# Moving batch 2's u transposes from TensorE to the DMA crossbar in a fused attention and mixer kernel

## The chip, the cores and the metric

The kernel runs on one core of one Trainium2 chip. The metric is the device time of one execution in microseconds (us), measured several times. A profiled execution gives a trace as well. A run counts as "slow" when it is over 1.5% above the fastest of the same kernel, else as "fast"; nearly all runs here are fast, and single runs are of unknown state. The granted clock of the core is recorded with each run; the text names it where a run of a changed kernel had 0.995 or less. The rounds ran on several chips, and the kernel before was timed anew in each.

Engines in the profile: PE is TensorE (matmuls), PEld its weight loads, DVE is VectorE, ACT is ScalarE, POOL is GpSimd, SP is SyncE. Here SP only issues DMAs; "SPq" and "POOLq" are the queues from which SP and GpSimd issue them. L748 is line 748 of the kernel.

## The reference, cut to what matters

The eight batches have 576 tokens of 512 features (8 heads of 64). First comes causal attention with a window of 64, then a low-rank mixer over the sequence, then a two-layer perceptron over the features:

```python
# attention of each batch and head, window 64, then x = heads side by side
xt = x.transpose(0, 2, 1)
h  = xt @ U @ V                       # rank 32, along the sequence
u  = x + h.transpose(0, 2, 1)         # (8, 576, 512)
ch = np.maximum(u @ w_ch1, 0.0) @ w_ch2   # 512 -> 2048 -> 512
return (u + ch).astype(np.float32)
```

In the kernels here the first product of the perceptron reads u with features on the partitions, that is, each 128x512 tile of u transposed.

## The kernel before: the parts that matter

The 8 x 576 tokens are cut into nine chunks of 512 tokens (four tiles of 128). A chunk is a list of 32 slots of perceptron work on PE: slots 0 to 15 each make one 128-row piece of the first product (`ch1`), slots 16 to 31 a quarter of one tile of the second (`ch2`). A slot is about 0.87 us of PE. Between slots, PE does the attention of a later batch; tables say after which slot each part goes. In chunk 1 this is batch 2, and its u (tiles 9 to 12) is read by chunk 2 (tiles 8 to 11) and chunk 3 (tile 12 onwards).

```python
    NXT = 3            # from this batch on, u is transposed by the crossbar
    ...
        def UT(t):
            def f():
                g = g0 + t
                dst = uT_of(g // TPC)[:, g % TPC, :, :]
                if b >= NXT:
                    nc.sync.dma_start_transpose(out=dst, in_=u_tiles[g][:])
                    return
                tp = ps_tp.tile([P, NDC, P], BF16, name="tpu", tag="tp")
                for dc in range(NDC):
                    nc.tensor.transpose(
                        tp[:, dc, :], u_tiles[g][:, dc * P : (dc + 1) * P], ident[:]
                    )
                nc.scalar.copy(out=dst, in_=tp[:])
            return f

```

`UT` either issues a crossbar transpose from SP or makes four PE transposes into the one-buffer PSUM pool `ps_tp`, with a copy on ACT. Batches 0 to 2 use PE in this kernel.

```python
        def ch1(*ids):
            def f():
                if len(ids) == 1:
                    ps = {ids[0]: psum["mm"].tile([P, CH], FP32, name="psA", tag="mm")}
                else:
                    pair = ps_big.tile([P, 2, CH], FP32, name="psA", tag="big")
                    ps = {i: pair[:, n, :] for n, i in enumerate(ids)}
                parts = (slice(0, TPC - 1), slice(TPC - 1, TPC)) if (c, ids) == (1, (0,)) else (slice(0, TPC),)
                for ts in parts:
                    for dc in range(NDC):
                        for i in ids:
                            nc.tensor.matmul(
                                ps[i][:, ts.start * P : ts.stop * P],
                                w1b[:, dc, i * P : (i + 1) * P],
                                uTc[:, ts, dc, :],
                                start=(dc == 0),
                                stop=(dc == NDC - 1),
                            )
                for i in ids:
                    c1[i] = c1_pool.tile([P, CH], BF16, name=f"c1_{i}")
                    if i in DVE_RELU.get(c, DVE_RELU_N):
                        nc.vector.tensor_relu(out=c1[i][:], in_=ps[i][:])
                    else:
                        nc.scalar.activation(out=c1[i][:], in_=ps[i][:], func=ACT.Relu)
            return f

        acc = {}
```

```python
    PLACE_2 = {                     # batch 2, in the slots of chunk 1
        "S": [9, 9, 9, 12, 12],     # scores, exp on ACT
        "M": [9, 10, 11, 13, 14],   # masks on DVE
        "SV": [15, 15, 16, 16],     # shifted copies of v on ACT and DVE
        "PV": [18],                 # values
        "U": [23],                  # x @ U
        "V": [24],                  # ... @ V, and u = x + h on DVE
        "UT": [27, 28, 29, 30],     # u transposed, tiles 9, 10, 11, 12
    }
    CROSS = {                       # q and k of a batch, transposed by the crossbar (SP)
        0: {2: [16, 17, 18, 19, 20]},
        1: {3: [10, 11, 12, 13, 14], 4: [26, 27, 28, 29, 30]},
        ...
```

In the traces here SP issues its DMAs in the order of the program (in u2, below, a u tile from a V product at 85.02 us went out at 98.64, behind four transposes that stand before it). The loads of q, k and v are issued by GpSimd and cast to bf16. In chunk 1 they are held until a crossbar transpose of batch 3 has landed (in the profile of the kernel before, GpSimd stands 8.91 us for it, until 81.92 us):

```python
            def loads(b, *tiles):
                for t in tiles:          # GpSimd copies one element, so it waits
                    nc.gpsimd.tensor_copy(out=held[:], in_=qfs[(b + 1) % 2][0:1, ...])
                if b <= 2:
                    load_v(b + 1)        # batch 3's v ...
                for _ in load_kq(b + 2, False):
                    pass                 # ... then batch 4's k and q
            ...
            if b == 2:
                slots[15].append(lambda: loads(2, 2))
```

The softmax here doesn't subtract the row's maximum and nothing guards it: scores larger than these inputs give would overflow.

Of the kernel before, what the change touches and what calls it, by code (L numbers as in the profile page):

```python
# [16 lines left out]
def kernel(  # L17
# [12 lines left out]
    B, H, S, D = q.shape  # L30
# [10 lines left out]
    GR = 6  # L41
    NGR = 2
    NXB = 2
    NXT = 3
    GP = S // GR
    NFULL = S // P
    CH = 512
    TPC = CH // P
# [199 lines left out]
    def uT_of(c):  # L248
        if c not in uT_tiles:
            uT_tiles[c] = uT_pool.tile([P, TPC, NDC, P], BF16, name="uTc")  # L250
        return uT_tiles[c]


    def attention(b, spare=False):
# [389 lines left out]
# [6 lines that stand above are left out]
# [53 lines left out]
        return pcs  # L703


    DVE_RELU = {0: (7, 9, 11, 15), 1: (4, 7, 9, 10, 11, 13, 14)}
    DVE_RELU_N = (0, 1, 2, 4, 5, 6, 8)

    def mlp(c):
        uTc = uT_of(c)  # L710
        c1 = [None] * NFC
# [5 lines that stand above are left out]
                else:  # L717
                    pair = ps_big.tile([P, 2, CH], FP32, name="psA", tag="big")
                    ps = {i: pair[:, n, :] for n, i in enumerate(ids)}
                parts = (slice(0, TPC - 1), slice(TPC - 1, TPC)) if (c, ids) == (1, (0,)) else (slice(0, TPC),)  # L720
                for ts in parts:
                    for dc in range(NDC):
                        for i in ids:
# [17 lines that stand above are left out]
        def ch2(t, quarter, parts=((0, DM),)):  # L741
            def f():
                g = c * TPC + t
                for lo, hi in parts:
                    if quarter == 0 or len(parts) > 1:
                        acc[t] = psum["mm"].tile([P, DM], FP32, name="psU", tag="mm")
                    for i in range(4 * quarter, NFC if len(parts) > 1 else 4 * quarter + 4):
                        nc.tensor.matmul(  # L748
                            acc[t][:, lo:hi],
                            c1[i][:, t * P : (t + 1) * P],  # L750
                            w2b[:, i, lo:hi],
                            start=(i == 0),
                            stop=(i == NFC - 1),
                        )
                    if quarter < 3 and len(parts) == 1:
                        continue
                    if c < NLATE:
                        osb = late[c * TPC + t]
                    else:
                        osb = out_pool.tile([P, DM], FP32, name="osb")  # L760
                    nc.vector.tensor_tensor(  # L761
                        out=osb[:, lo:hi],
                        in0=acc[t][:, lo:hi],
                        in1=u_tiles[g][:, lo:hi],
                        op=ALU.add,
                    )
                    if c < NLATE:
                        stores.append(
                            lambda: nc.sync.dma_start(
                                out=outf[g * P : (g + 1) * P, :], in_=osb[:]  # L770
                            )
                        )
                        continue
                    nc.sync.dma_start(out=outf[g * P : (g + 1) * P, lo:hi], in_=osb[:, lo:hi])
            return f

        ups = [ch1(i) for i in range(NFC)]
        if c == 0:
            ups[0:2] = [ch1(0, 1), lambda: None]
            rest = [ch2(t, r) for r in range(4) for t in (0, 1)]  # L780
            return ups + rest + [ch2(t, r) for t in (2, 3) for r in range(4)]
        rest = [ch2(t, r) for t in range(TPC) for r in range(4)]
        if c == NCH - 1:
            rest[-4:] = [ch2(TPC - 1, 0, ((0, 3 * P), (3 * P, DM)))]
        return ups + rest
# [19 lines left out]
        "UT": [28, 29, 30, 31, 102],  # L805
    }
    PLACE_2 = {
        "S": [9, 9, 9, 12, 12],
        "M": [9, 10, 11, 13, 14],
        "SV": [15, 15, 16, 16],  # L810
        "PV": [18],
        "U": [23],
        "V": [24],
        "UT": [27, 28, 29, 30],
    }
    PLACE_3 = {**PLACE, "SV": [5, 5, 6, 6]}
    CROSS = {
# [182 lines left out]
```

## Time and profile before

| | before |
|---|---|
| time, median of 3 (lowest to highest) | 312.85 us (312.75 to 312.92) |
| span in the profile | 311.4 us |
| PE busy | 303.9 us, 98% |
| chain of waits | 93% PE |
| chunk 2's first matmul | 92.67 us |

The page's first part gives the span, then busy time, share of the span and number of instructions for each engine:

```profile
span 311.4 us, 6970 instructions
...
PE 303.9 (98%) x2897; PEld 148.4 (48%) x2919; DVE 161.8 (52%) x308; ACT 108.8 (35%) x173; POOL 101.7 (33%) x133
```

The second view is the list of PE's waits between 59 and 125 us, where chunks 1 and 2 lie. Its columns are engine and line, what was waited for, total us, times, longest:

```profile
PE psU L748 <- issue: 0.2, 1, 0.2
```

PE waits for nothing there but 0.2 us of its own issue. So the kernel gets faster only by taking work from PE, and any new wait of PE counts in full.

The timeline (start, duration, engine, line, operation, how many) shows what one group of PE transposes costs. Groups of four second-layer matmuls with transposes between them start 1.085 us apart (1.09 us from 88.54 to 89.63, and the same twice more until 91.80); four such matmuls alone take 0.865 us:

```profile
88.32 0.39 PE L653 MATMUL tpu<-ident,un 128*128 128x128 bf16 x4
88.54 1.03 PE L748 MATMUL psU<-w2b,c 128*128 128x512 bf16 x4
89.41 0.39 PE L653 MATMUL tpu<-ident,un 128*128 128x128 bf16 x4
89.63 1.03 PE L748 MATMUL psU<-w2b,c 128*128 128x512 bf16 x4
...
91.80 1.03 PE L748 MATMUL psU<-w2b,c 128*128 128x512 bf16 x4
92.67 0.59 PE L724 MATMUL psA<-uTc,w1b 128*128 128x512 bf16 x2
```

SP's timeline shows when its queue is taken. The last q/k transpose of batch 3 goes out at 83.16. Batch 3's u, which already uses the crossbar here, goes out from 112.93:

```profile
83.16 1.22 SPq L304 DMA_TRANSPOSE qf<-qr  x1
...
112.93 5.89 SPq L649 DMA_TRANSPOSE uTc<-un  x4
```

Landing times (issue to the DMA's completion) are given by the view of one tile in a window. First the k transpose issued at 81.86, just before GpSimd's first load of the next group (82.46); then batch 3's u, issued from 112.93 to 119.5 beside GpSimd's loads:

```profile
L304 SPq DMA_TRANSPOSE kf<-kr x1: 1207/1207/1207, 81.9 to 81.9; - x1
...
DMA to landing us min/median/max: 2.5/2.5/2.5
```

```profile
DMA to landing us min/median/max: 6.4/7.4/8.0
```

GpSimd's timeline tells when those loads begin in chunk 1. Batch 3's v starts at 82.46 (four loads) and 85.93, and batch 4's k and q follow at once:

```profile
82.46 3.52 POOL L137 DMA_DIRECT2D vA<-in_v_dram  x4 [0.36 <-DVE rco L506]
85.93 0.92 POOL L137 DMA_DIRECT2D vB<-in_v_dram  x1
86.79 0.93 POOL L128 DMA_DIRECT2D kr<-in_k_dram  x1
```

### The profile page before, as it was taken

How to read it: one execution, taken by the hardware profiler on the slowest of the kernel's cores; microseconds unless marked ns; L12 is line 12 of the kernel's file. 1: busy time of each engine (PE TensorE's matmuls, PEld its weight loads, DVE VectorE, ACT ScalarE, POOL GpSimd, SP SyncE). 2: the span in 40 equal slices, each digit the busy share in tenths (PEclk: the TensorE clock that was granted, in tenths of full speed). 3: DMA queues.
4: the chain of work that ended last, by engine and by line, in shares of the span. 5: the costliest groups of instructions: out<-in, count | busy, mean ns of one | idle time of the engine just before them, and what ended most of it. 6: DMA issues, size and time to landing. Idle time of an engine off the chain costs nothing.

```text
span 311.4 us, 6970 instructions
## 1 busy us (share of the span) xinstructions
PE 303.9 (98%) x2897; PEld 148.4 (48%) x2919; DVE 161.8 (52%) x308; ACT 108.8 (35%) x173; POOL 101.7 (33%) x133
## 2 busy tenths in 40 slices
PE   8989999999999999999999999999999999999996
PEld 7643554544455544453445344544454444444443
DVE  4665467437758753774368435844574343016011
ACT  3745670467038510642063304340345003201500
POOL 8693263293497097029308710000000000000000
PEclk9999999999999999999999999999999999999999
DMA  7999999999999999999999999515100545010012
GB/s 108 167 210 208 205 168 147 145 148 154 129 150 140 126 152 156 182 161 159 163 155 207 150 106 181 128 48 133 69 2 0 120 180 193 27 76 34 0 64 73
DMA packets 156496, 39.88 MB, mean 128 GB/s; under 512 B 145040, under 2 KB 151440, under 8 KB 156464
## 3 DMA queue, kind: packets, MB, share of 16 engines
q0 software_dynamic: 104720, 18.88, 87.3%
q1 hardware_dynamic: 51744, 20.55, 35.0%
q8 instruction: 23, 0.38, 0.5%
q14 instruction: 9, 0.07, 0.1%
HBM read 37.97 MB, written 9.44 MB: 152 GB/s over the span
## 4 chain that ended last, share of the span: by engine, by line
PE 93%; DMA 3%; POOL 2%; issue 1%; ACT 0%; DVE 0%; POOLq 0%
PE psA L724 41%; PE psU L748 40%; DMA vA<-in_v_dram 3%; PE sc L345 3%; PE xw L407 2%; PE psv L619 2%; PE pshh L531 1%; PE tpu L653 1%; PE tpg L281 0%; POOL qr L119 0%; PE low L345 0%; PE psh L531 0%; POOL vB L151 0%; PE xr L407 0%; POOL kr L119 0%
## 5 line engine op out<-in xcount | busy, mean ns | idle before, releaser
L724 PE MATMUL psA<-uTc,w1b 128*128 128x512 bf16 (+1 forms) x580 | 131.2, 378 | 0.4 <-ACT uTc L599 0.4
L748 PE MATMUL psU<-w2b,c 128*128 128x512 bf16 (+2 forms) x572 | 127.5, 373 | 1.3 <-issue 0.3
L748 PEld LDWEIGHTS <-c 128*128 128x128 bf16 x592 | 56.0, 98 | 66.4 <-issue 3.6
L724 PEld LDWEIGHTS <-w1b 128*128 128x128 bf16 x580 | 54.1, 98 | 64.4 <-issue 2.9
L736 ACT ACTIVATE c<-psA 128x512 bf16<-128x512 f32 x84 | 50.0, 597 | 88.3 <-PE psA L724 88.0
L761 DVE TENSOR_TENSOR osb<-psU,un 128x512 f32<-128x512 f32 (+2 forms) x29 | 19.5, 672 | 69.3 <-PE psU L748 69.3
L734 DVE TENSOR_SCALAR c<-psA 128x512 bf16<-128x512 f32 x60 | 41.3, 688 | 25.6 <-PE psA L724 25.6
L634 DVE TENSOR_TENSOR un<-psv,xs 128x512 bf16<-128x512 f32 (+3 forms) x48 | 26.1, 592 | 23.5 <-PE psv L619 23.3
L365 ACT ACTIVATE pts<-sc 128x1024 bf16<-128x1024 f32 x32 | 31.4, 1028 | 2.3 <-PE sc L345 2.3
L137 POOL DMA_DIRECT2D vA<-in_v_dram x32 | 28.5, 915 | 8.1 <-DMA w1b<-in_moe_w_ch_dram 2.8
L128 POOL DMA_DIRECT2D qr<-in_q_dram x30 | 26.7, 890 | 4.5 <-DMA w2b<-in_moe_w_ch_dram 3.1
L128 POOL DMA_DIRECT2D kr<-in_k_dram x30 | 26.7, 890 | 4.1 <-PE psA L724 2.0
L398 ACT ACTIVATE ptl<-low 128x256 bf16<-128x256 f32 x6 | 2.3, 384 | 62.0 <-PE high L345 62.0
L371 DVE TENSOR_TENSOR pts<-pts,maskA 128x1024 bf16<-128x1024 bf16 x28 | 19.1, 682 | 1.7 <-ACT pts L365 1.7
L922 POOL COPY held<-qf 1x1 bf16<-1x1 bf16 x5 | 1.1, 228 | 54.0 <-DMA qf<-qr 54.0
L498 DVE TENSOR_TENSOR xs<-xw,rcw 128x896 bf16<-128x896 f32 x14 | 15.3, 1091 | 0.5
L345 PEld LDWEIGHTS <-kf 64*64 64x64 bf16 x704 | 9.9, 107 | 7.7 <-issue 7.0
L345 PE MATMUL sc<-qf,kf 64*64 64x128 bf16 (+1 forms) x608 | 11.7, 212 | 0.5 <-DVE qf L298 0.3
L407 PEld LDWEIGHTS <-pts 128*64 128x64 bf16 x512 | 9.9, 110 | 3.7 <-issue 3.2
L546 ACT CAST hh<-pshh 128x512 bf16<-128x512 f32 x7 | 4.1, 586 | 13.7 <-PE pshh L539 13.5
L656 ACT COPY uTc<-tpu 128x512 bf16<-128x512 bf16 x9 | 5.3, 585 | 10.2 <-PE tpu L653 10.2
L407 PE MATMUL xw<-vA,pts 128*64 128x65 bf16 x217 | 8.4, 195 | 0.0
(115 smaller groups left out, 175.3 us busy)
## 6 DMA issues: line engine op xcount, KB each, us to landing
out_dram<-osb SPq DMA_DIRECT2D x27, 256.0 KB, 2.3
vA<-in_v_dram POOLq DMA_DIRECT2D x32, 128.0 KB, 8.1
kr<-in_k_dram POOLq DMA_DIRECT2D x24, 128.0 KB, 5.8
qr<-in_q_dram POOLq DMA_DIRECT2D x24, 128.0 KB, 6.4
w2b<-in_moe_w_ch_dram POOLq DMA_DIRECT2D x4, 512.0 KB, 15.0
out_dram<-late SPq DMA_DIRECT2D x8, 256.0 KB, 3.0
vB<-in_v_dram POOLq DMA_DIRECT2D x8, 128.0 KB, 12.3
w1b<-in_moe_w_ch_dram POOLq DMA_DIRECT2D x2, 512.0 KB, 11.5
```

The costliest lines, as they stand in the source:

```text
L128: nc.gpsimd.dma_start(out=dst[0:rows, t, :, :], in_=src[b, :, t * P : t * P + rows, :].rearrange("h p d -> p h d"),)
L137: nc.gpsimd.dma_start(out=dst[:, :, 0:D], in_=v[b, :, lo : lo + P, :].rearrange("h p d -> p h d"))
L345: nc.tensor.matmul(sc[g][r0 : r0 + W, col * W : (col + n) * W], keys_of(j, u, rs), queries_of(j, blk, n, rs), start=not spare, stop=last o ...
L365: nc.scalar.activation(out=dst, in_=sc[:], func=ACT.Exp, scale=scale)
L371: nc.vector.tensor_tensor(out=dst, in0=dst, in1=maskA.rearrange("p g n w -> p g (n w)"), op=ALU.mult)
L407: nc.tensor.matmul(dst, pts[:, h // 2, h % 2, blk, :] if blk < NB - 1 else ptl[:, h // 2, h % 2, :], rhs, start=True, stop=True,)
L634: nc.vector.tensor_tensor(out=u_tiles[g][rs, cs], in0=ps[0][n][rs], in1=x[rs, t, :, :].rearrange("p h d -> p (h d)")[:, cs], op=ALU.add,)
L724: nc.tensor.matmul(ps[i][:, ts.start * P : ts.stop * P], w1b[:, dc, i * P : (i + 1) * P], uTc[:, ts, dc, :], start=(dc == 0), stop=(dc == ...
L734: nc.vector.tensor_relu(out=c1[i][:], in_=ps[i][:])
L736: nc.scalar.activation(out=c1[i][:], in_=ps[i][:], func=ACT.Relu)
L748: nc.tensor.matmul(acc[t][:, lo:hi], c1[i][:, t * P : (t + 1) * P], w2b[:, i, lo:hi], start=(i == 0), stop=(i == NFC - 1),)
L761: nc.vector.tensor_tensor(out=osb[:, lo:hi], in0=acc[t][:, lo:hi], in1=u_tiles[g][:, lo:hi], op=ALU.add,)
```

## The change

The intent is to take batch 2's sixteen transposes off PE. The transposes then go through SP and need some microseconds to land (batch 3's u tiles took 6.4 to 8.0 us in the profile before), so batch 2's attention is moved forward in chunk 1: scores by one slot, values and both low-rank products by three, and the u transposes to slots 22 and 23, ahead of batch 4's q/k transposes (slot 26 on) in SP's order. Chunk 2's first product is split so that the first three tiles need not wait for the fourth. The fourth tile of chunk 2 is batch 2's third u tile, tile 11.

```diff
--- before.py
+++ after.py
@@ -41,7 +41,7 @@
     GR = 6
     NGR = 2
     NXB = 2
-    NXT = 3
+    NXT = 2
     GP = S // GR
     NFULL = S // P
     CH = 512
@@ -703,7 +703,7 @@
         return pcs
 
 
-    DVE_RELU = {0: (7, 9, 11, 15), 1: (4, 7, 9, 10, 11, 13, 14)}
+    DVE_RELU = {0: (7, 9, 11, 15), 1: (3, 6, 8, 9, 10, 12, 13)}
     DVE_RELU_N = (0, 1, 2, 4, 5, 6, 8)
 
     def mlp(c):
@@ -717,7 +717,7 @@
                 else:
                     pair = ps_big.tile([P, 2, CH], FP32, name="psA", tag="big")
                     ps = {i: pair[:, n, :] for n, i in enumerate(ids)}
-                parts = (slice(0, TPC - 1), slice(TPC - 1, TPC)) if (c, ids) == (1, (0,)) else (slice(0, TPC),)
+                parts = (slice(0, TPC - 1), slice(TPC - 1, TPC)) if c in (1, 2) and ids == (0,) else (slice(0, TPC),)
                 for ts in parts:
                     for dc in range(NDC):
                         for i in ids:
@@ -805,13 +805,13 @@
         "UT": [28, 29, 30, 31, 102],
     }
     PLACE_2 = {
-        "S": [9, 9, 9, 12, 12],
-        "M": [9, 10, 11, 13, 14],
-        "SV": [15, 15, 16, 16],
-        "PV": [18],
-        "U": [23],
-        "V": [24],
-        "UT": [27, 28, 29, 30],
+        "S": [8, 8, 8, 11, 11],
+        "M": [8, 9, 10, 12, 13],
+        "SV": [13, 13, 14, 14],
+        "PV": [15],
+        "U": [20],
+        "V": [21],
+        "UT": [22, 22, 23, 23],
     }
     PLACE_3 = {**PLACE, "SV": [5, 5, 6, 6]}
     CROSS = {
```

## The prediction

> **What bounds the kernel now.** TensorE. The page gives PE 303.9 us busy of a 311.4 us span (98%), at full granted clock in all 40 slices; the chain of waits is 93% PE. From chunk 0 on nothing makes PE wait: in the waits of 56 to 135 us the largest wait of a PE matmul is 0.2 us. So the time changes only by PE work removed or by a new hole in PE.
>
> **Removed.** For batch 2, sixteen 128x128 PE transposes and four ACT copies (585 ns each). In the timeline, groups of four second-layer matmuls with a transpose group between them start 1.085 us apart (88.54, 89.63, 90.72, 91.80) against 0.865 us for four such matmuls alone. So a group costs PE 0.22 us, four of them **0.88 us**, all on the critical path. The ACT copies are off it.
>
> **Added.** Four crossbar transposes on the SP queue, about 1.47 us of queue each (four of batch 3's took 5.89 us). Splitting chunk 2's first product (384 + 128 columns) costs almost nothing: the split one in chunk 1 runs as fast; I allow 0.05 us.
>
> **Moved.** Scores and masks one slot sooner, values, first low-rank product and V product three, relus one. The shift copies of v then end close to where the values start on PE (about 75 us); I allow 0.1 us.
>
> **The new critical question: do the transposes land before chunk 2 starts?** V's product moves from 85.07 to about 82.5 us, so the first u tile of batch 2 is added at about 84.1. But SP issues batch 3's ten q/k transposes back to back until 84.4, so batch 2's u goes out at about 84.5, 85.9, 87.4 and 88.9. Chunk 2 needs the first two for its first part, the third for its second; without PE's transposes it would start at 92.67 - 0.88 = 91.8. Landing takes 2.5 us [...] (the k transpose at 81.86), but GpSimd's loads of batch 4 begin at 82.46 and fill the engines from about 85: the q transpose of 83.16 took 5.4, and batch 3's u at 112.9 to 117.3, in the like situation, took 6.4, 7.0, 8.0, 7.4. [...] My estimate is 6, 6.5, 7: landings at 90.5, 92.4, 94.4. PE then stalls about 0.6 us for the second tile, runs the 0.65 us first part, and stalls another 1.0 us or so for the third. About 1.5 us (0 to 3) lost against 0.88 saved.
>
> Later: batch 4's loads and transposes are pushed by 1 to 2 us of DMA work; they have about 8 us before chunk 3 reads them. Batch 3's u transposes have 1.6 us of slack; they should just hold.
>
> **Time.** 312.85 - 0.88 + 0.05 + 0.1 + 1.3 (stall, weighed slightly low) = **313.4 us**, 8 in 10 within **312.0 to 314.7**. Faster by over 2%: 0.01; within 2%: 0.98; slower by over 2%: 0.01.
>
> **What would show it.** Right: the transpose group falls from 36 matmuls to 20; the u transposes on SP rise from 23 to 27, the new ones issued from about 84.5 us, just behind batch 3's, landing in 5.5 to 8 us; new PE waits for a DMA at chunk 2's first product, 1 to 2 us together. Wrong: landings near 4 us and no PE wait there (then 312.0).
>
> **What would make it wrong.** Landings faster or slower by 1 us move the result by up to 2 us; a later u add on DVE; batch 3's u transposes delayed enough to stall chunk 3.

312.85 - 0.88 + 0.05 + 0.1 + 1.3 = 313.42, stated as 313.4 us. The landings of 6, 6.5 and 7 us stay the estimate from the measured 6.4 to 8.0 us. In the trace of the kernel before, the transpose that took 2.5 us went out at 81.86 us and GpSimd's next load at 82.46; the time of all packets over that of 16 engines was 0.48 from 81.0 to 82.5 us, 0.44 to 84.0, 0.87 to 85.0 and 1.84 to 86.0.

## The result, and the profile after

| | before | after |
|---|---|---|
| time, median of 6 (lowest to highest) | 312.88 us (312.75 to 313.72) | 314.87 us (314.58 to 315.13) |
| ratio of the fast runs | | 1.0059, 95% interval 1.0046 to 1.0072 |
| span of the profiled execution | 311.4 us | 312.9 us |
| chunk 1, first matmul to chunk 2's first | 33.36 us | 33.32 us |
| chunk 2, the same | 32.04 us | 33.49 us |
| each of chunks 3 to 6 | 32.04 to 32.05 us | 32.04 to 32.05 us |

A ratio is the mean time of one kernel's fast runs over that of the other's of the same rounds, so it is not quite the ratio of the medians quoted. A chunk's time is the distance between the first matmuls of two chunks in the trace. The sum of chunks 1 and 2 is 65.40 us before and 66.81 after: +1.41 us. Nothing after chunk 2 differs. Another 0.24 us lies after the last DVE addition (2.72 us to the span's end before, 2.96 after), which no view explains. It belongs to the program and not to one run: in all twelve traces of kernels with NXT = 2 this end takes 2.95 to 2.97 us, in those of u1 and u8 (NXT = 3) 2.71 and 2.72, in u12 and u13 2.60 and 2.59. Chunk 1 began 0.16 us earlier in this trace, so the spans differ by 1.5 us.

The page:

```profile
span 312.9 us, 6954 instructions
...
PE 303.2 (97%) x2886; PEld 147.4 (47%) x2907; DVE 161.6 (52%) x308; ACT 106.5 (34%) x169; POOL 101.4 (32%) x133
```

PE's u transposes fell from 36 matmuls to 20 and the u transposes on SP rose from 23 to 27, as forecast. PE's waits between 59 and 125 us now have a new first line. PE waited twice for a transposed u tile:

```profile
PE psA L724 <- DMA uTc<-un: 1.9, 2, 1.3
```

PE's timeline shows both waits in brackets. V's product is at 82.42. The second layer of chunk 1 ends, then PE stands until tiles 9 and 10 have landed, runs the first part (384 columns), and stands again for tile 11:

```profile
82.42 0.71 PE L619 MATMUL psv<-hh,vrep 64*128 64x256 bf16 x6
83.06 8.81 PE L748 MATMUL psU<-w2b,c 128*128 128x512 bf16 x39
92.47 0.81 PE L724 MATMUL psA<-uTc,w1b 128*128 128x384 bf16 x4 [0.59 <-DMA uTc<-un]
94.56 0.38 PE L724 MATMUL psA<-uTc,w1b 128*128 128x128 bf16 x4 [1.28 <-DMA uTc<-un]
```

The bracketed waits understate the loss, because ends of matmuls are modelled and weight loads wait too (those of L724 stood 2.6 us between 90 and 96 us). The chunk times give it better. Without waits, chunk 1 would take 33.36 - 0.88 (transposes gone) + 0.11 (the earlier placement, measured below) = 32.59 us; it took 33.32, so the first wait cost 0.73. Chunk 2 took 33.49 against 32.04, so the second cost 1.45. The sum is 2.18 us, and -0.88 + 0.11 + 2.18 = 1.41, by construction. The starts of the matmuls check it: the holes are 0.97 and 1.61 us from one start to the next, where 0.22 and 0.16 us are usual, so 0.75 and 1.45 us too long.

SP's timeline: batch 2's u goes out immediately behind batch 3's last q transpose:

```profile
82.88 1.22 SPq L304 DMA_TRANSPOSE qf<-qr  x1
84.19 5.54 SPq L649 DMA_TRANSPOSE uTc<-un  x4
94.24 1.19 SPq L304 DMA_TRANSPOSE kf<-kr  x1
```

The landing of the u tiles (three of the four are recorded):

```profile
DMA to landing us min/median/max: 6.7/7.5/8.1
```

The chain of waits between 80 and 96 us (start, us, what) runs from the additions on DVE over SP's queue to the DMA that ends the second wait:

```profile
83.08 2.80 DVE un L634 x5
...
86.48 0.40 SPq L649
...
86.98 7.54 DMA uTc<-un
...
94.56 0.38 PE psA L724 x4
```

And GpSimd's loads, in the same place as before (those of k and q follow from 86.13):

```profile
81.80 3.52 POOL L137 DMA_DIRECT2D vA<-in_v_dram  x4 [0.36 <-PE pshh L539]
```

### The profile page after: what moved, and what is told of

It reads as the page before. It is cut to its first block, busy times and chain, and to the rows that moved or that the text cites. A ratio compares the mean times of both kernels' runs of the same rounds, so it can differ in the third digit from the quotient of the medians.

```text
span 312.9 us, 6954 instructions
## 1 busy us (share of the span) xinstructions
PE 303.2 (97%) x2886; PEld 147.4 (47%) x2907; DVE 161.6 (52%) x308; ACT 106.5 (34%) x169; POOL 101.4 (32%) x133
## 4 chain that ended last, share of the span: by engine, by line
PE 89%; DMA 5%; POOL 2%; DVE 1%; issue 1%; ACT 0%; SPq 0%; POOLq 0%
PE psA L724 41%; PE psU L748 37%; DMA vA<-in_v_dram 3%; PE sc L345 2%; DMA uTc<-un 2%; PE xw L407 2%; PE psv L619 2%; PE pshh L531 1%; DVE un L634 1%; PE tpg L281 0%; POOL qr L119 0%; PE low L345 0%; PE psh L531 0%; POOL vB L151 0%; PE tpu L653 0%
## 5 line engine op out<-in xcount | busy, mean ns | idle before, releaser
L724 PE MATMUL psA<-uTc,w1b 128*128 128x512 bf16 (+1 forms) x584 | 131.3, 377 | 2.3 <-DMA uTc<-un 1.9
L724 PEld LDWEIGHTS <-w1b 128*128 128x128 bf16 x584 | 54.3, 98 | 66.7 <-issue 5.5
L137 POOL DMA_DIRECT2D vB<-in_v_dram x8 | 7.2, 896 | 6.4 <-DMA kr<-in_k_dram 3.6
L761 DVE TENSOR_TENSOR late<-psU,un 128x512 f32<-128x512 f32 x8 | 5.4, 686 | 6.9 <-PE psU L748 6.8
```

Of the source, the lines that this page charges most:

```text
L137: nc.gpsimd.dma_start(out=dst[:, :, 0:D], in_=v[b, :, lo : lo + P, :].rearrange("h p d -> p h d"))
L724: nc.tensor.matmul(ps[i][:, ts.start * P : ts.stop * P], w1b[:, dc, i * P : (i + 1) * P], uTc[:, ts, dc, :], start=(dc == 0), stop=(dc == ...
L761: nc.vector.tensor_tensor(out=osb[:, lo:hi], in0=acc[t][:, lo:hi], in1=u_tiles[g][:, lo:hi], op=ALU.add,)
```

## The experiments

The theory ("landing"): PE waits for the landing of tiles 10 and 11, and the landing takes 7 us because GpSimd's loads are under way beside it. Rival 1 ("placement"): the earlier attention and the split cost PE time through DVE and ACT. Rival 2 ("queue"): a u transpose takes 7 us anyway, so only the late issue matters. All kernels gave correct results. Each was timed in 5 rounds against the kernel before, except where said; with the profiled run that makes six times (five for u10). "Chunks 1+2" is from the trace, to be compared with 65.40 us before and 66.81 after.

### u1: PE transposes again, everything else of the change kept

```diff
-    NXT = 2
+    NXT = 3
```

> The change with batch 2's u transposed by PE again (placement and split kept). Landing theory (PE waits for the crossbar at chunk 2's start): no wait for a DMA there, 312.9 us, ratio 1.000 within 0.001. Rival (earlier placement and split cost PE time through DVE, ACT or shorter matmuls): stays well slower than before, near 314.9 plus 0.9 of transposes, about 315.7.

Measured: 315.29 us (315.04 to 315.61), before 313.16, ratio 1.0058 (1.0029 to 1.0086). Chunks 1+2: 67.39 us. This missed the expectation, and taken alone it would have favoured rival 1. PE's timeline shows why it is no clean undo:

```profile
84.44 0.40 PE L653 MATMUL tpu<-ident,un 128*128 128x128 bf16 x4
85.51 0.38 PE L653 MATMUL tpu<-ident,un 128*128 128x128 bf16 x4 [0.67 <-ACT uTc L656]
```

The same comes again at 86.60 and 87.66.

Two groups of transposes stand in one slot. The second needs the only buffer of `ps_tp`, which ACT has to empty first, so PE waits 0.67 us twice in the brackets; from group start to group start it is 1.07 us, against 0.22 us for a group. Undoing one part left the others arranged for something else. So the run does not decide between the theories; u8 is the mended version.

### u8: PE transposes in their old slots, attention early, product split

```diff
-    NXT = 2
+    NXT = 3
-        "UT": [22, 22, 23, 23],
+        "UT": [27, 28, 29, 30],
```

> The earlier placement of batch 2's attention and the split alone: the u transposes back on PE and in their old slots (27 to 30), where the first such run had put them right behind V's product and PE waited for the additions and for the single PSUM buffer. Landing theory: nothing of the loss is left, 312.9 to 313.1 us (0.1 us for the placement). Rival (the placement costs): still 314 or more.

Measured: 313.17 us (312.94 to 315.83; the slowest at a granted clock of 0.995), before 313.26, ratio 1.0012 (0.9986 to 1.0037). Chunks 1+2: 65.51 us, 0.11 more than before, and no wait of PE for a DMA. So the placement and the split together cost 0.11 us. Rival 1 falls.

### u2: the crossbar alone, old placement, no split

```diff
-    NXT = 3          # in the kernel before
+    NXT = 2
```

> The kernel before with the crossbar for batch 2's u only: old placement, no split. Landing theory: V's product stays at about 85 us, so the u transposes are issued from about 86.7 and the third, that the unsplit first product needs, lands at about 89.7 + 7 = 96.7, against 91.6 for PE: stall 5 us, less 0.9 saved, so about 317 us. Rival (placement and split are what costs): 312.0 to 312.5.

Measured: 334.49 us (333.91 to 335.51, granted clock 0.967 to 0.969), before 313.16, ratio 1.0673. The direction was the landing theory's, the size four times its 5 us. PE waited 19.7 us in one piece:

```profile
PE psA L724 <- DMA uTc<-un: 19.7, 1, 19.7
```

SP's timeline shows what the expectation had overlooked. In the old slots 27 to 30 the u transposes (L649) stand in SP's program in turn with batch 4's q/k transposes (L304), behind the first two pairs of them, and those wait for batch 4's loads:

```profile
95.46 1.41 SPq L304 DMA_TRANSPOSE kf<-kr  x1
96.96 1.59 SPq L304 DMA_TRANSPOSE qf<-qr  x1
98.64 1.31 SPq L649 DMA_TRANSPOSE uTc<-un  x1
100.05 1.32 SPq L304 DMA_TRANSPOSE kf<-kr  x1
```

V's product was at 85.02 us, but the first u tile went out at 98.64 and the third at 107.71. In this trace SP stood 7.6 us at the first of batch 4's transposes (issued at 92.83 us) until its load had landed, with every later DMA of its queue behind it. The trace then grants half the clock for 20.5 us from 95.9 us on, which adds to the 334 us. What the change's move to slots 22 and 23 buys is thus above all a place in SP's order (u9 tests this).

### u9: old attention slots, u transposes before batch 4's in SP's order

```diff
-    NXT = 3          # in the kernel before
+    NXT = 2
-        "UT": [27, 28, 29, 30],
+        "UT": [25, 25, 25, 25],
+ # and chunk 2's first product split, as in the change
```

> Crossbar for batch 2's u and the split, batch 2's attention in its old slots, but its u transposes put before batch 4's q and k transposes in SP's order (slot 25), which the crossbar-alone run had not done. If that run's 20 us came of SP's order, the first u goes out at about 86.7 us, the third lands at about 97, PE waits 4 to 5 us, perhaps with some microseconds at half clock after it: 316.5 to 318.5 us. If the order was not the cause: 330 or more.

Measured: 318.94 us (317.90 to 320.19, granted clock 0.988 to 0.995), before 313.10, ratio 1.0183 (1.0159 to 1.0207). That is a little above the 316.5 to 318.5 us expected. One wait, of the length expected:

```profile
PE psA L724 <- DMA uTc<-un: 4.0, 1, 4.0
```

So about 15 of u2's 21 us came of SP's order and the half clock that followed (u9 has the split besides), and the earlier attention is worth about 4 us more (318.94 against 314.87, with different sets of runs on different chips; u9 too has 3.4 us at about half clock after its wait, 0.52 from 95.3 to 98.7 us).

### u3: the change without the split

```diff
-  ... if c in (1, 2) and ids == (0,) else ...
+  ... if (c, ids) == (1, (0,)) else ...
```

> The change with chunk 2's first product in one piece. Landing theory: the first three-tile part (0.65 us) no longer runs in the wait for the third tile, so 0.65 us slower than the change: 315.5. Rival (the split itself costs): 314.6 or less.

Measured: 317.33 us (316.64 to 318.94), before 313.16, ratio 1.0132 (1.0096 to 1.0167). The direction is right, but it lost far more than 0.65 us against the change. All six runs had a granted clock of 0.988 to 0.995. The wait is one piece of 2.0 us, and the windows around it (us, length, busy time and count for PE, PEld, DVE, ACT, POOL, then the granted clock, the time of all DMA packets over that of 16 engines, which can pass 1, and GB/s) show half the clock for 3.4 us after it:

```profile
PE psA L724 <- DMA uTc<-un: 2.0, 1, 2.0
```

```profile
91.00:95.30 4.30, 2.28 (x11) 0.77 (x9) 0.69 (x1) 0.00 (x0) 3.34 (x5) 1.00 2.08 152
95.30:98.70 3.40, 3.40 (x58) 1.83 (x58) 1.27 (x3) 2.49 (x4) 2.28 (x4) 0.50 2.30 155
```

The distance from the last matmul's start to the next was 2.40 us in this hole. The change has two holes of 0.97 and 1.61 us instead, with 0.65 us of matmuls between, and its trace has full clock. From the landing of tile 11 to chunk 3 it took 33.72 us against 31.44 in the change: 0.65 us for the first part, as expected, and most of the rest in chunk 2 at half clock (33.58 us against 32.04). The split uses the wait, and here the clock stayed full with it. In these traces the length of the hole alone does not decide: the 2.40 us hole here was followed by half the clock and a 2.11 us hole in u10 left it full, while in c3's head half the clock (0.50 from 14.6 to 18.0 us) followed holes of at most 1.89 us (10.68 to 12.57). What else decides is not shown.

### u5: batch 4's k and q held until batch 2's third u tile has landed

Batch 3's v is loaded early, right behind batch 3's k and q (about 73 us), so no load stands beside the u transposes. The bytes are the same.

```diff
-                if b <= 2:
+                if b == 1:
                     load_v(b + 1)
                 for _ in load_kq(b + 2, False):
                     pass
+                if b == 1:
+                    load_v(b + 2)
 ...
+                    if b == 2:                    # GpSimd waits for tile 11 of u
+                        last = uT_of(2)[0:1, 3, 0, 0:1]
-                slots[15].append(lambda: loads(2, 2))
+                slots[24].append(lambda: loads(2, 2))
```

> The change with the loads of batch 4's k and q held on GpSimd until batch 2's third u tile has landed, and batch 3's v loaded before instead, right behind its k and q; the same bytes, another order. Landing theory (GpSimd's loads slow the transposes): the u transposes land in 2.5 to 4 us instead of 6.7 to 7.5, the wait at chunk 2's start falls under 0.5 us, 312.0 to 312.4 us. Rival (a u transpose takes 7 us anyway, or its late issue on the SP queue is what counts): landing stays near 7 and the time near 314.9.

Measured: 313.23 us (312.80 to 314.82; the slowest at a clock of 0.995), before 313.16, ratio 0.9997 (0.9965 to 1.0029). The landing of all four u tiles:

```profile
DMA to landing us min/median/max: 2.4/2.8/3.8
```

PE does not wait for u any more; the eight matmuls of the split product follow each other:

```profile
92.03 1.04 PE L724 MATMUL psA<-uTc,w1b 128*128 128x384 bf16 x8
```

The u transposes went out later than in the change (86.03 against 84.19: from the first of batch 3's q/k transposes to the first u tile SP took 16.31 us against 14.32 in the change, with v's loads issued beside them, from 72.89 to 77.41; in u4, which moves v alike, the u tiles went out from 85.75) and still the third landed at 91.13 instead of 94.52. So it was the loads and not the issue: rival 2 falls. By what mechanism the loads slow the landing is not shown. While the u tiles were under way the packets' time over that of the 16 engines was 2.04 in the change (84.2 to 92.3 us) and 1.07 here (86.0 to 92.4), but the bytes moved were 149 and 161 GB/s: GB/s alone would not have told that the landing would be slow. A second trace agrees: in u2 batch 3's u tiles, issued from 134.04 with no load of GpSimd under way, landed in 2.4 to 2.6 us.

The time came out about 1 us above the expected 312.0 to 312.4. Chunks 1+2 take 65.24 us: chunk 1 32.79 (0.20 above the 32.59 without waits), chunk 2 32.45 (0.41 above 32.04). The moved loads now run while DVE makes its shifted copies of v. Groups by line and shape, in the same part of chunk 2, first before, then here (count, busy us, mean ns, idle):

```profile
L151 DVE COPY vB<-vA 64x520 bf16<-64x520 bf16 x3 | 0.8, 277 | 0.0
```

```profile
L151 DVE COPY vB<-vA 64x520 bf16<-64x520 bf16 x3 | 1.2, 431 | 0.0
```

The same copies take 431 ns instead of 277 while GpSimd issues, and PE waits 0.2 us for one of them. In the kernel before, GpSimd's last load there was issued by 100.25 us and these copies began at 100.50; here two of them, from 101.38 on, stand beside loads issued from 100.06 to 101.91 and take 0.84 us together, against 0.48 before. Why a copy is slower beside them is not shown. The trace places all of the 0.6 us at these copies' reader, the value products: from the first to the last of them (`xw`) PE takes 1.34 us in chunk 1 against 1.10 in the change, and 1.37 us in chunk 2 against 1.00 before. No run takes the overlap away; u10 was meant to and did not.

### u4: batch 3's v early, batch 4's k and q not held (control for u5)

The first half of u5's edit, without the hold.

> Control for the first gated run: batch 3's v loaded early as there, but batch 4's k and q not held, so they start at about 82 to 83 us as v did in the change. Landing theory: u tiles land in 5.5 to 8 us, PE waits 1.5 to 3 us at chunk 2, 314.3 to 315.2 us. Rival (it was the early v, not the held loads, that took the wait away): no wait, near 313.2.

Measured: 314.63 us (313.86 to 316.05), before 313.10, ratio 1.0052 (1.0028 to 1.0076). Chunks 1+2: 66.86 us. PE waits again (1.6 us in the list), and the landing is

```profile
DMA to landing us min/median/max: 4.8/5.4/6.6
```

The landing is a little shorter than the 5.5 to 8 us expected, the wait and the time are as expected. Loading v early does not help by itself; k and q beside the transposes are enough to slow them.

### u10: v where the change has it, k and q held until the first u tile has landed

```diff
                 if b <= 2:
                     load_v(b + 1)
+                if b == 2:                        # GpSimd waits for tile 9 of u
+                    nc.gpsimd.tensor_copy(out=held[:], in_=uT_of(2)[0:1, 1, 0, 0:1])
                 for _ in load_kq(b + 2, False):
 ...
-                slots[15].append(lambda: loads(2, 2))
+                slots[23].append(lambda: loads(2, 2))
```

> The change with batch 4's k and q loads held until batch 2's first u tile has landed; batch 3's v is loaded where the change loads it, so GpSimd issues nothing while VectorE and ScalarE copy v. Landing theory: u tiles land in 3 to 5 us, PE's wait at chunk 2 under 0.3 us, and without the slowed copies of the first gated run 312.0 to 312.4 us. Rival (landing does not depend on these loads): near 314.9.

Measured: 314.52 us (313.99 to 314.91), before 313.26, ratio 1.0040 (1.0027 to 1.0052). The expectation was wrong. The five loads of v, issued from 83.36 to 87.7, kept the landing long. Tile 9 landed after 6.4 us, at 91.43, before k's first load went out (92.07); the other three landed with k and q partly beside them:

```profile
DMA to landing us min/median/max: 5.3/6.3/7.1
```

PE waited 1.7 us in one piece, for tile 10. Its distance from matmul to matmul was 2.11 us, and here the clock stayed at 1.0 in all runs. Nor were the copies of v spared: k and q now ran beside those in chunk 2 (448 ns on average). Together u4, u5 and u10 say that either set of loads is enough to slow the transposes, and that of these versions only the one with neither (u5) lands the u tiles in 2.4 to 3.8 us.

### u14: batch 3's first scores moved in front of chunk 2's first product

```diff
-    PLACE_3 = {**PLACE, "SV": [5, 5, 6, 6]}
+    PLACE_3 = {**PLACE, "S": [3, 3], "SV": [5, 5, 6, 6]}
+            if c == 1:
+                slots[31] += att[3]["S"][:3]
+                att[3]["S"] = att[3]["S"][3:]
```

> The change with the first three groups of scores of batch 3 moved from after chunk 2's first product to before it (slot 31 of chunk 1): the same PE work, some 0.9 us of it now inside the wait. Landing theory: the wait for the second tile disappears, the third tile's landing still ends the hole, and the time falls by 0.8 to 1.0 us against the change, to about 314.0. Rival (a fixed restart or displacement cost): no faster than the change, 314.9 or more.

Measured: median 314.82 us (313.80 to 318.63; two runs at a clock of 0.993 and 0.994, one of them slow), before 313.33, ratio 1.0053 (1.0005 to 1.0100). The times do not show the expected gain. The trace shows half of it: chunks 1+2 take 66.31 us, and relative to the landing of tile 11 (next entry) that is 0.55 us less than in the change. The first wait shrank to 0.2 us. This is inconclusive in time and supports the theory in the trace.

### c1, c2, c3: the change again

c1 is timed in 5 rounds; c2 and c3 are single looks (state unknown).

> The change itself once more, as a control on this chip and for a second profile. Every theory: about 314.9 us. Landing theory: again two PE waits for u tiles before chunk 2's first product, 2 to 3 us together, with the second and third u tile landing 6.5 to 8 us after issue.

> The change, third profile. Landing theory: third u tile lands 7 to 8 us after issue and 35.3 to 36 us after chunk 1 starts, and chunks 1 and 2 together are longer than in the kernel before by the landing's excess: 1.3 to 2.0 us.

> The change, fourth profile; as the third. If the landing moves by some tenths of a microsecond from profile to profile and the chunks' time moves with it, the landing sets the size.

Measured: c1 315.75 us (314.31 to 316.72; two runs at a clock of 0.995 and 0.993), before 313.26, ratio 1.0078 (1.0055 to 1.0100); c2 314.89; c3 315.56. With the first profile of the change there are four traces of it:

| profile | tile 11 lands, after chunk 1's first matmul | chunks 1+2 | more than before | chunks 1+2 minus landing |
|---|---|---|---|---|
| after | 94.52 - 59.15 = 35.37 us | 66.81 us | 1.41 us | 31.44 us |
| c1 | 94.82 - 58.95 = 35.87 us | 67.31 us | 1.91 us | 31.44 us |
| c2 | 94.83 - 59.61 = 35.22 us | 66.66 us | 1.26 us | 31.44 us |
| c3 | 95.50 - 60.66 = 34.84 us | 66.28 us | 0.88 us | 31.44 us |

The last column, the time from tile 11's landing to chunk 3's first matmul, is constant to 0.01 us. So in these traces the landing of tile 11 sets the loss, one for one, and this instant moves by 1 us from run to run: its issue by 0.65 us (27.57 to 28.22 after chunk 1's first matmul) and its time to land by 0.39 (7.26 to 7.65). c1's time was above the expected 314.9, and the losses of c2 and c3, 1.26 and 0.88 us, lie under the expected 1.3 to 2.0. c3's slow time has another cause: its trace grants half the clock for 3.4 us in the kernel's head, before chunk 0 (0.50 from 14.6 to 18.0 us).

Some runs of the kernel before had a reduced clock as well (315.33 us at 0.995 and 316.09 at 0.989 in these rounds).

### u12, u13 and u7: is there a version that beats both?

u12 and u13 are one kernel, run twice: the kernel before, with only tile 8 (batch 1's last) and tile 12 (batch 2's last) by the crossbar. Tile 8 has 30 us until chunk 2 reads it; tile 12 is read by chunk 3.

```diff
-                if b >= NXT:
+                if b >= NXT or g in (8, 12):
```

> The kernel before, with only the two u tiles by the crossbar whose readers come late: tile 8 (batch 1's last, issued 30 us before chunk 2) and tile 12 (batch 2's last, read by chunk 3 only). Landing theory: no wait at all and two groups of PE transposes (0.22 us each) saved: 0.4 us faster than before, ratio 0.9986. Rival (a crossbar transpose of u costs something else): same or slower than before.

> The two-tile version (tiles 8 and 12 by the crossbar, else the kernel before) once more, for a second set of times: 0.3 to 0.4 us faster than before, ratio 0.9988, apart from runs in which the granted clock dips.

Measured: 312.92 us (312.41 to 315.17), before 313.26, ratio 0.9998 (0.9972 to 1.0024); and 312.79 us (312.50 to 315.40), before 313.10, ratio 1.0011 (0.9981 to 1.0040). In both traces chunk 1 takes 32.91 us, 0.45 less than before: two groups of transposes at 0.22 us, as costed, and PE has no new wait. Chunks 1+2 take 65.09 and 65.00 us against 65.40. But three of the twelve runs had a clock of 0.995 and took 314.25 to 315.40 us, so in the means the gain is not there, and the intervals contain 1. Whether those runs are bad luck is open.

u7 is u5 with tile 8 by the crossbar too:

```diff
+                if b >= NXT or g == 8:    # on top of u5
```

> The first gated run (batch 3's v early, batch 4's k and q after the third u tile) with batch 1's last u tile, tile 8, by the crossbar too. Landing theory: no wait for a u tile; 0.22 us faster than the first gated run, so 312.6 to 313.0, ratio 0.999.

Measured: 313.45 us (312.86 to 313.86), before 313.10, ratio 1.0005 (0.9990 to 1.0020). Batch 2's u transposes were issued from 87.14 us, about 1 us later than in u5, and PE waited 0.2 us for one. No gain: chunks 1+2 take 65.63 us against 65.24 in u5. No version here is shown to beat the kernel before.

## Why the prediction was wrong

The prediction said 313.4 us (312.0 to 314.7). The median was 314.87, just outside.

1. **What bounds the kernel: right.** PE had no slack, and each new wait of PE appears in the time.
2. **0.88 us saved: right.** u12's two removed groups shortened chunk 1 by 0.45 us.
3. **0.05 + 0.1 us for split and placement: right.** u8 measured 0.11 us for both.
4. **When the u transposes are issued: right.** Predicted 84.5 us behind batch 3's q/k transposes; measured 84.19 in the same place.
5. **Landing "6, 6.5, 7": a little short.** In the trace the second took 6.7 us and the third 7.5, but the third was issued earlier (86.98 against 87.4), so it landed at 94.52 against the predicted 94.4. The reason, GpSimd's loads, is shown by u5.
6. **The stall: here the prediction failed.** The step read: "PE then stalls about 0.6 us for the second tile, runs the 0.65 us first part, and stalls another 1.0 us or so for the third. About 1.5 us (0 to 3) lost against 0.88 saved", and the sum then took 1.3 us ("stall, weighed slightly low"). Its own landings gave more: tile 10 at 92.4, first part until 93.05, tile 11 at 94.4, hence 1.35 us for the second wait and 1.95 in all. The trace shows 0.73 us (predicted 0.6) and 1.45 us (predicted 1.0), 2.18 us together, in the first profile, and the four profiles of the change, less 32.59 + 32.04 us, give 1.65 to 2.68. So the two waits were foreseen, and the mis-sized term is the stall: 1.3 us against 2.2. With 1.95 the sum would have been 312.85 - 0.88 + 0.05 + 0.1 + 1.95 = 314.07 us, still 0.8 below the median; point 8 has the rest as far as it is known. Also, a landing later by 1 us costs 1 us and not "up to 2 us": the four profiles have a constant time from tile 11's landing on.
7. **Later chunks: right.** Chunks 3 to 6 are unchanged; batch 3's u transposes, issued 1.25 us later, arrive in time.
8. **Not predicted:** 0.24 us more after the last addition, seen in the trace and not explained, and the spread of the landing. The first profiled execution was also the fastest of its six; the other five took 0.17 to 0.55 us more. (That of the kernel before took 313.08 us, 0.20 above its median, so the two traces differ by 1.5 us where the medians differ by 2.0.) The four profiles show that landing differences of this size exist, but those five were not traced, so for them this is an inference.

## What to carry to other kernels

Moving a transpose from a saturated engine to a DMA turns work into a deadline: compare the last landing (issue in queue order, plus the landing time under the load that will be there: a 128x512 bf16 tile issued from SP took 2.4 to 3.8 us in u5, where k and q were held until the third tile had landed, and 4.8 to 8.1 us beside GpSimd's loads in u4, u10 and the change) with the instant at which the reader arrives, and add up the two waits exactly instead of rounding them towards hope. Move first the tiles whose readers come late. Look at the program order of the queue that issues it, since in u2 a DMA that waited 7.6 us for its data held up all behind it (PE waited 19.7 us), and break an unavoidable wait into pieces with some work between: in u3 the one longer hole, of 2.40 us, was also followed by half the clock.
